# Layer norm's scales made later on POOL, stored 17 steps behind the residual sum, and read back in a stage of their own

## The chip, the core and the metric

The kernel runs on one core of one Trainium2 chip. The metric is the device time of one execution in microseconds. A core has TensorE (PE, matmuls), VectorE (DVE), ScalarE (ACT), GpSimd (POOL) and SyncE (SP), which here only issues transfers. Each engine works through its own instructions in the order in which the program emits them, so an instruction that waits holds all that stand behind it on its engine.

## What is computed

A transformer block on 2048 tokens of width 1024 in fp32: layer norm, linear attention with a learned feature map (32 heads of 32), output projection `wo` and residual sum; then layer norm, an up projection to 3584, ReLU, a down projection and a second residual sum.

```python
x = A_x
h = x + _A_ref(_layernorm(x, axis=-1), A_wqkv, A_w_phi, A_wo)
h2 = h + _B_ref(_layernorm(h, axis=-1), B_w1, B_w2)

def _layernorm(x, axis=-1, eps=1e-5):
    m = jnp.mean(x, axis=axis, keepdims=True)
    v = jnp.var(x, axis=axis, keepdims=True)
    return (x - m) / jnp.sqrt(v + eps)

def _B_ref(x, w1, w2):
    h = jnp.maximum(jnp.einsum("bsd,df->bsf", x, w1), 0)
    return jnp.einsum("bsf,fd->bsd", h, w2)
```

The case is about the second layer norm, that of `h`.

## The kernel before, in words

**Precision.** Every large operand is split into a high and a low part, and each product is three matmuls (`mm3`, L181 to L183). ACT makes the high part of a weight (L124), DVE or POOL the low part (L128).

**Order of work.** The program is a list of *items*, each some matmul groups: the key and value projections, the query projections, 32 items of the output projection (`wo_item`, 8 steps each), then the items of the up projection (4 steps each) and of the down projection. A *step* is one group of three matmuls. Everything beside the matmuls is put into a table by hand: `when(step, f, ...)` emits `f` behind the matmuls of that step. What stands under one step keeps the order in which it was entered: attention first, then the output projection, then the layer norm. `Units.advance` adds weight loads and splits at each step, as buffers come free. Below, steps are counted from the first item of the output projection; the up projection begins at step 256.

**Attention beside the output projection.** Units of the attention go two by two every 16 steps. SP loads both units' features (`at_load`, L528, tile qe: steps 63, 79, 95, 111, 127, 143, 159). POOL multiplies them with the sums of keys (L560, tile ez), DVE reduces (L566), POOL makes denominators (L576, L580), DVE inverts (L583), POOL scales (L593, L598), DVE transposes (L604), and TensorE multiplies with the key-value matrix (`at_num`, L618: steps 62, 78, 94, 110, 126 and so on; the transposes stand 10 and 7 steps before). ACT copies the result out as the high part (L625), DVE makes the low part (L636), into oT, from which the output projection reads four tiles of 128 tokens at a time.

**Output projection.** Item n of 32 is one tile and one half of the 1024 columns. SP loads that part of `x` (L643, tile xh, four buffers), DVE adds it to the product (L669) at step 8n + 9, and takes statistics of it (L680, L683). SP stores the sum to DRAM (L672, tile hd) at 8n + 14. With a tile's second half, POOL makes the layer norm's scale and bias (`ln_power`, L230 to L232) two steps behind the sum, and SP stores these two numbers per token (`wo_scale`, L688, tile scd) five steps behind the sum.

**Second layer norm.** `ln_pair` takes two tiles of tokens, 512 apart. Stage 0: for each tile and each of four groups of 32 partitions, SP reads back the scales (L698, tile scx, 1 KB) and then the rows in another layout (L699, tile xin, 128 KB); sixteen transfers in turn. Tile xin has two buffers. Stage 1: ACT applies scale and bias, four instructions for each tile (L706). Stages 2 and 3: DVE transposes each tile (L709). Stage 4: DVE makes a sum and a difference of the two tiles (L713, L714). Stage 5: POOL makes two more (L718, L719). Then `ln_store` stores seven arrays (L728, tile hs), the inputs of the up projection's seven products. `h_load` reads them (L736, tile hT), ACT and DVE split them (L744, L748).

There are eight pairs. The four of the first 1024 tokens (b = 0) run beside the output projection, pair i from step 64 + 40 i on; the four others (b = 1) beside the first half of the up projection, pair i from 60 + 68 i behind its start. The offsets of the stages are in `LN2`: with (5, 14, 18, 20, 22, 24, 30), pair 0 loads at 69, goes through ACT at 78, DVE at 82, 84 and 86, POOL at 88 and is stored from 94 to 97.

**Up projection.** Each item multiplies one weight block with one of the seven inputs into a bank of PSUM; ACT drains some banks (L771), DVE adds others (L774), then ACT and DVE do the ReLU and the combinations (L777, L780, L783), and SP stores them (L786).

Of the kernel before, what the change touches and what calls it, by code (L numbers as in the profile page):

```python
# [139 lines left out]
def kernel(  # L140
# [12 lines left out]
    v, act, pool, pe, sp = nc.vector, nc.scalar, nc.gpsimd, nc.tensor, nc.sync  # L153
# [34 lines left out]
    def do(n, k, f, *args):  # L188
        at[n, k].append((f, args))
# [8 lines left out]
    scd = [dram.tile([P, 2], F32, name=f"scd{t}") for t in range(NT)]  # L198
# [9 lines left out]
    xin, xst, xnt = {}, {}, {}  # L208
# [481 lines left out]
    def ln_pair(b, i, stage):  # L690

        tiles = [HT * b + 4 * r + i for r in range(2)]
        if stage == 0:
            for r, t in enumerate(tiles):
                xnt["h", t] = x = lnp.tile([P, D], F32, name="xin")
                for a in range(4):
                    rows = slice(32 * a, 32 * (a + 1))
                    sp.dma_start(scx[rows, 2 * i + r], scd[t].rearrange("(g t) s -> t g s", g=4))  # L698
                    sp.dma_start(x[rows].rearrange("p (c g k) -> p c g k", c=8, g=4),  # L699
                                 hd[t].rearrange("(g t) (c a k) -> a t c g k", g=4, a=4, k=32)[a])  # L700
        elif stage == 1:
            for r, t in enumerate(tiles):
                x = xnt["h", t].rearrange("p (c g k) -> p c g k", c=8, g=4)
                for g in range(4):
                    sc = scx[:, 2 * i + r, g]
                    act.activation(x[:, :, g], x[:, :, g], AF.Identity, bias=sc[:, 1:2], scale=sc[:, 0:1])  # L706
        elif stage in (2, 3):
            x = xnt["h", tiles[stage - 2]]
            v.transpose(x, x)  # L709
        elif stage == 4:  # L710
            x1, x2 = (xnt["h", t] for t in tiles)
            sums[b, i] = s12 = (mp or hp).tile([P, 2, 512], F32, name="s12", bufs=1)
            v.tensor_add(s12[:, 0, :], x2[:, 0:512], x2[:, 512:])  # L713
            v.tensor_sub(x2[:, 0:512], x1[:, 0:512], x2[:, 0:512])  # L714
        elif stage == 5:
            x1, s12 = xnt["h", tiles[0]], sums[b, i]
            s4 = (mp or hp).tile([P, 512], F32, name="s4l", bufs=1)
            pool.tensor_tensor(out=s12[:, 1, :], in0=s12[:, 0, :], in1=x1[:, 0:512], op=ALU.subtract)  # L718
            pool.tensor_tensor(out=s4, in0=x1[:, 512:], in1=s12[:, 1, :], op=ALU.subtract)  # L719
            sums[b, i] = s12, s4  # L720
# [178 lines left out]
    def when(step, f, *args):  # L899

        if step < 8 * first_up:
            do(step // 8, step % 8, f, *args)
        else:
            do(first_up + (step - 8 * first_up) // 4, step % 4, f, *args)
# [138 lines left out]
    for (t, hf), n in order:  # L1043
        do(max(n - 1, wo_first), -1, wo_load, t, hf)
        added = 8 * n + (11 if n < wo_first + 2 else 9)
        when(added, wo_add, t, hf)
        when(added, wo_stats, t, hf)
        if hf == 1:
            when(added + 2, ln_power, ("h", t))
            when(added + 5, wo_scale, t)  # L1050
        when(8 * n + (10 if n > order[-3][1] else 14), wo_store, t, hf)

    LN2 = ((5, 14, 18, 20, 22, 24, 30), (0, 14, 20, 24, 28, 32, 42))
    wo0 = 8 * wo_first
    up0 = 8 * first_up
    for i in range(4):
        for stage in range(6):
            when(wo0 + 64 + 40 * i + LN2[0][stage], ln_pair, 0, i, stage)  # L1060
            when(up0 + 60 + 68 * i + LN2[1][stage], ln_pair, 1, i, stage)
        for j in range(7):
            when(wo0 + 64 + 40 * i + LN2[0][6] + j // 2, ln_store, 0, i, j)
            when(up0 + 60 + 68 * i + LN2[1][6] + j, ln_store, 1, i, j)
    assert wo_n[8, 0] + 10 < first_up

    def up_step(b, p, m):
# [53 lines left out]
    scx = consts.tile([P, HT, 4, 2], F32, name="scx")  # L1121
# [16 lines left out]
    for i in range(4):  # L1138
        r = slice(32 * i, 32 * (i + 1))
# [76 lines left out]
```

## Time and profile before

| | us |
|---|---|
| median of 3 runs | 1953.69 |
| lowest, highest | 1952.56, 1957.18 |
| the profiled execution | 1965.29 |
| its span, first to last instruction | 1963.5 |
| its mean granted TensorE clock | 0.985 of full speed |

The profile is one execution, recorded by the hardware. Each line of its groups gives the source line, the engine, the operation and the names of the tiles as out<-in. A line of the waits reads: who waited <- for whom: us in total, times, longest. A line of the timeline gives start, duration, engine, line and tiles, and in brackets how long the engine was idle before and what ended that. SPq is SP's queue, whose durations are those of issuing a transfer and not of the transfer. A wait for several things is put down to the one that came last.

### The profile page before, as it was taken

The page shows a single profiled execution, that of the slowest core. Times are in us where ns is not written, and L with a number is a line of the kernel's source. Part 1 is how long each engine was busy: PE and PEld are TensorE (multiplying, and loading weights), DVE is VectorE, ACT ScalarE, POOL GpSimd, SP SyncE. Part 2 cuts the span into 40 slices and gives each one's busy share as a digit, 9 for nine tenths or more (in the row PEclk, how much of TensorE's full clock was granted, in tenths as well). Part 3 has the DMA queues.
Part 4 walks back from the last instruction along what each step waited for, and adds up shares of the span by engine and source line. Part 5 has one row for each costly group of instructions (what it writes and reads, how often), then busy time and mean ns, then how long its engine had stood idle before and what let it go on. Part 6 is the DMA issues. An engine that isn't in the chain of part 4 may idle for free. (4 is left out here: it accounts for less than half of the span.)

```text
span 1963.5 us, 31404 instructions
## 1 busy us (share of the span) xinstructions
PE 1902.4 (97%) x11288; PEld 1559.5 (79%) x11288; DVE 1058.3 (54%) x1673; ACT 754.0 (38%) x1334; POOL 969.6 (49%) x961
## 2 busy tenths in 40 slices
PE   9999999999999988978999999999999999999999
PEld 7888788877787766757777888888888888888887
DVE  6666578667589866455444655443343343334333
ACT  5433335222233121134444555444444444444442
POOL 4776752889856867432322322222244444444443
PEclk9999999999999989989999999999999999999999
DMA  6888786666675687797878897665677677877765
GB/s 219 272 272 266 229 272 208 196 196 196 198 236 164 176 188 174 176 256 212 238 223 242 267 305 220 198 210 175 195 247 220 209 217 235 259 215 216 214 215 177
DMA packets 368475, 432.22 MB, mean 220 GB/s; under 512 B 102208, under 2 KB 228160, under 8 KB 368320
## 3 DMA queue, kind: packets, MB, share of 16 engines
q1 hardware_dynamic: 351424, 413.45, 70.5%
q10 hardware_dynamic: 16896, 16.78, 2.5%
q8 instruction: 88, 1.44, 0.3%
q14 instruction: 67, 0.55, 0.1%
HBM read 292.75 MB, written 137.38 MB: 219 GB/s over the span
## 5 line engine op out<-in xcount | busy, mean ns | idle before, releaser
L128 POOL TENSOR_TENSOR w<-raw,w 128x512 fp32r<-128x512 f32 x355 | 473.1, 1334 | 751.9 <-ACT w L124 700.0
L124 ACT ACTIVATE w<-raw 128x512 fp32r<-128x512 f32 x686 | 409.2, 626 | 475.6 <-PE mm L183 212.0
L128 DVE TENSOR_TENSOR w<-raw,w 128x512 fp32r<-128x512 f32 x331 | 274.9, 831 | 545.2 <-ACT w L124 537.3
L181 PE MATMUL mm<-w,xT 128*128 128x512 f32 x768 | 311.0, 405 | 0.0
L182 PE MATMUL mm<-w,xT 128*128 128x512 f32 x768 | 300.7, 392 | 4.6 <-POOL w L128 3.5
L183 PE MATMUL mm<-w,xT 128*128 128x512 f32 x768 | 299.7, 390 | 0.0
L181 PE MATMUL mm<-hT,w 128*128 128x512 f32 x672 | 266.2, 396 | 24.4 <-ACT hT L744 11.1
L182 PE MATMUL mm<-hT,w 128*128 128x512 f32 x672 | 265.5, 395 | 3.2 <-DVE hT L748 3.2
L183 PE MATMUL mm<-hT,w 128*128 128x512 f32 x672 | 264.7, 394 | 0.0
L348 POOL TENSOR_TENSOR b<-b 128x256 f32<-128x256 f32 x224 | 181.5, 810 | 89.9 <-DMA b<-in_w_dram 73.8
L182 PEld LDWEIGHTS mm<-w,xT 128*128 128x128 f32 x768 | 144.5, 188 | 36.0 <-POOL w L128 6.8
L181 PEld LDWEIGHTS mm<-hT,w 128*128 128x128 f32 x672 | 128.4, 191 | 54.3 <-ACT hT L744 11.9
L181 PEld LDWEIGHTS mm<-w,xT 128*128 128x128 f32 x768 | 144.4, 188 | 30.6 <-issue 1.8
L183 PEld LDWEIGHTS mm<-w,xT 128*128 128x128 f32 x768 | 144.2, 188 | 30.7
L182 PEld LDWEIGHTS mm<-hT,w 128*128 128x128 f32 x672 | 128.3, 191 | 31.0 <-DVE hT L748 4.2
L181 PE MATMUL mm<-w 128*128 128x512 f32 x392 | 152.5, 389 | 0.0
L182 PE MATMUL mm<-w 128*128 128x512 f32 x392 | 152.5, 389 | 0.0
L183 PE MATMUL mm<-w 128*128 128x512 f32 x392 | 152.5, 389 | 0.0
L183 PEld LDWEIGHTS mm<-hT,w 128*128 128x128 f32 x672 | 128.4, 191 | 26.9
L183 PEld LDWEIGHTS mm<-w 128*128 128x128 f32 x392 | 73.6, 188 | 15.3
L182 PEld LDWEIGHTS mm<-w 128*128 128x128 f32 x392 | 73.6, 188 | 15.3
L181 PEld LDWEIGHTS mm<-w 128*128 128x128 f32 x392 | 73.6, 188 | 15.2
(159 smaller groups left out, 3147.0 us busy)
## 6 DMA issues: line engine op xcount, KB each, us to landing
raw<-t SPq DMA_DIRECT2D x224, 256.0 KB, 4.2
raw<-ad SPq DMA_DIRECT2D x196, 256.0 KB, 3.0
raw<-in_w_dram SPq DMA_DIRECT2D x168, 256.0 KB, 3.1
b<-in_w_dram SPq DMA_DIRECT2D x56, 512.0 KB, 4.1
t<-b SPq DMA_DIRECT2D x56, 512.0 KB, 4.3
ad<-c SPq DMA_DIRECT2D x112, 256.0 KB, 3.5
ad<-s SPq DMA_DIRECT2D x84, 256.0 KB, 4.1
ed<-qe ACTq DMA_DIRECT2D x32, 512.0 KB, 4.9
```

Source lines behind the costliest of these rows:

```text
L124: nc.scalar.activation(w[:, 0, :], raw[1], AF.Copy)
L128: eng.tensor_tensor(out=w[:, 1, :], in0=raw[1], in1=w[:, 0, :].bitcast(F32), op=ALU.subtract)
L181: pe.matmul(ps, a_hi, b_hi, start=first, stop=False, skip_group_check=more)
L182: pe.matmul(ps, a_hi, b_lo, start=False, stop=False, skip_group_check=more)
L183: pe.matmul(ps, a_lo, b_hi, start=False, stop=last, skip_group_check=more)
L348: pool.tensor_tensor(out=tsum[j, *out], in0=tsum[j, *a], in1=tsum[j, *b], op=ALU.subtract)
```

## The change

The scales are made four steps behind the sum instead of two, and stored 17 behind it instead of five. The pair's stage 0 loads only the rows; a new stage 1 loads the scales; the later stages are numbered one higher. For b = 0, pair 0 gets offsets of its own (rows at 70, scales 84, ACT 91, DVE 93, 94 and 96, POOL 97, stores 100 to 103), and the others begin five steps earlier and end six later (rows 0, scales 8, ACT 20, DVE 25, 27, 29, POOL 31, stores from 36). For b = 1 the scales are loaded 4 steps behind the rows, and everything from ACT on is four steps later.

```diff
                 for a in range(4):
                     rows = slice(32 * a, 32 * (a + 1))
-                    sp.dma_start(scx[rows, 2 * i + r], scd[t].rearrange("(g t) s -> t g s", g=4))
                     sp.dma_start(x[rows].rearrange("p (c g k) -> p c g k", c=8, g=4),
                                  hd[t].rearrange("(g t) (c a k) -> a t c g k", g=4, a=4, k=32)[a])
         elif stage == 1:
+            for r, t in enumerate(tiles):
+                for a in range(4):
+                    sp.dma_start(scx[32 * a:32 * (a + 1), 2 * i + r], scd[t].rearrange("(g t) s -> t g s", g=4))
+        elif stage == 2:
...
-            when(added + 2, ln_power, ("h", t))
-            when(added + 5, wo_scale, t)
+            when(added + 4, ln_power, ("h", t))
+            when(added + 17, wo_scale, t)
...
-    LN2 = ((5, 14, 18, 20, 22, 24, 30), (0, 14, 20, 24, 28, 32, 42))
+    LN2 = ((0, 8, 20, 25, 27, 29, 31, 36), (0, 4, 18, 24, 28, 32, 36, 46))
     wo0 = 8 * wo_first
     up0 = 8 * first_up
     for i in range(4):
-        for stage in range(6):
-            when(wo0 + 64 + 40 * i + LN2[0][stage], ln_pair, 0, i, stage)
+        first, ln2 = wo0 + 64 + 40 * i, LN2[0] if i else (6, 20, 27, 29, 30, 32, 33, 36)
+        for stage in range(7):
+            when(first + ln2[stage], ln_pair, 0, i, stage)
             when(up0 + 60 + 68 * i + LN2[1][stage], ln_pair, 1, i, stage)
         for j in range(7):
-            when(wo0 + 64 + 40 * i + LN2[0][6] + j // 2, ln_store, 0, i, j)
-            when(up0 + 60 + 68 * i + LN2[1][6] + j, ln_store, 1, i, j)
+            when(first + ln2[7] + j // 2, ln_store, 0, i, j)
+            when(up0 + 60 + 68 * i + LN2[1][7] + j, ln_store, 1, i, j)
```

More of the change, by code (lines that the diff above doesn't have):

```diff
@@ L706, in ln_pair @@
                     act.activation(x[:, :, g], x[:, :, g], AF.Identity, bias=sc[:, 1:2], scale=sc[:, 0:1])
-        elif stage in (2, 3):
-            x = xnt["h", tiles[stage - 2]]
+        elif stage in (3, 4):
+            x = xnt["h", tiles[stage - 3]]
             v.transpose(x, x)
-        elif stage == 4:
+        elif stage == 5:
             x1, x2 = (xnt["h", t] for t in tiles)
@@ L714, in ln_pair @@
             v.tensor_sub(x2[:, 0:512], x1[:, 0:512], x2[:, 0:512])
-        elif stage == 5:
+        elif stage == 6:
             x1, s12 = xnt["h", tiles[0]], sums[b, i]
```

## The prediction

> **What bounds the kernel now.** I read the page's head first: TensorE is busy for nearly the whole span.
>
> ```profile
> span 1963.5 us, 31404 instructions
> PE 1902.4 (97%) x11288; PEld 1559.5 (79%) x11288; DVE 1058.3 (54%) x1673; ACT 754.0 (38%) x1334; POOL 969.6 (49%) x961
> ```
>
> So the order and amount of matmuls set the end, and a change beside them is worth only what TensorE loses. The change touches no matmul; it must work through TensorE's gaps. The second view is the table of busy time in 20 us stretches (PE, PEld, DVE, ACT and POOL busy time, then granted clock, DMA share, GB/s). These six rows are those where TensorE is worst:
>
> ```profile
> 700.00:720.00 20.00, 14.03 (x144) 11.03 (x144) 11.05 (x19) 2.88 (x8) 10.85 (x14) 0.83 0.88 289
> 720.00:740.00 20.00, 17.34 (x295) 13.71 (x302) 13.05 (x23) 5.38 (x12) 13.98 (x19) 0.83 0.81 127
> 740.00:760.00 20.00, 14.95 (x109) 11.38 (x96) 13.72 (x23) 1.21 (x4) 18.07 (x23) 0.83 0.64 162
> ...
> 780.00:800.00 20.00, 15.89 (x179) 12.31 (x178) 11.06 (x16) 5.37 (x12) 12.03 (x15) 0.83 0.56 155
> ...
> 860.00:880.00 20.00, 12.73 (x42) 9.66 (x43) 10.57 (x15) 6.26 (x9) 10.00 (x16) 0.76 0.93 225
> 880.00:900.00 20.00, 15.04 (x57) 11.56 (x55) 5.32 (x6) 9.89 (x15) 3.95 (x5) 0.84 0.90 217
> ```
>
> There are two losses in each: TensorE stands idle, and its clock is granted at less than 1 for a while. All six lie where the output projection and the second layer norm run (to about 862 us) or where the up projection begins. The third view, TensorE's waits, names the causes, first from 620 to 860 us, then from 860 to 1130 us:
>
> ```profile
> PE tp L618 <- DVE qe L604: 12.0, 3, 6.3
> PE mm L183 <- DVE oT L636: 5.7, 2, 5.1
> ```
>
> ```profile
> PE mm L181 <- ACT hT L744: 11.1, 2, 8.3
> PE mm L181 <- DVE c L774: 6.3, 2, 4.2
> PE mm L181 <- DVE xh L669: 4.8, 1, 4.8
> PE mm L182 <- DVE hT L748: 3.2, 2, 2.7
> PE mm L181 <- ACT c L771: 2.2, 1, 2.2
> ```
>
> The attention's own products (L618) wait for a transpose on DVE, the projection for DVE's low parts, the up projection for its inputs hT. None of these is slow by itself; each is late because its engine or its load was queued behind the layer norm. Step by step, from the queue of SP (start, duration), the first pair of tiles:
>
> ```profile
> 681.11 0.42 SPq L698 DMA_DIRECT2D scx<-scd  x1
> ...
> 696.34 0.56 SPq L699 DMA_DIRECT2D xin<-hd  x1
> ...
> 699.16 1.09 SPq L528 DMA_DIRECT2D qe<-ed  x2
> ```
>
> Sixteen transfers, scales and rows in turn, hold SP for 696.34 + 0.56 - 681.11 = 15.8 us. Two things follow. The second tile's rows come last, so ACT and then DVE wait with everything behind them (ACT, then DVE):
>
> ```profile
> 699.59 2.07 ACT L706 ACTIVATE xin<-xin,scx 128x256 f32<-128x256 f32 x4 [3.28 <-DVE qe L604]
> ```
>
> ```profile
> 701.70 1.25 DVE L709 STREAM_TRANSPOSE xin<-xin 128x1024 f32<-128x1024 f32 x1 [2.98 <-ACT xin L706]
> ...
> 704.31 1.24 DVE L604 STREAM_TRANSPOSE qe<-qe 128x1024 f32<-128x1024 f32 x1
> ```
>
> DVE's L604, which L618 waits for, stands behind L709 in program order: this is the 6.3 us wait. And the qe load at 699.16 was behind the block, so POOL starved:
>
> ```profile
> 708.46 2.54 POOL L560 TENSOR_TENSOR ez<-qe,zb 128x512 f32<-128x512 f32 x2 [11.66 <-DMA qe<-ed]
> ```
>
> What POOL then does late makes the next transposes and L636 late. SP itself is held by POOL as well (SP's waits from 650 to 900 us):
>
> ```profile
> SPq L688 <- POOL qtz L576: 31.6, 4, 10.6
> SPq L643 <- DMA hd<-xh: 15.7, 8, 5.6
> SPq L688 <- POOL sc L232: 14.2, 4, 7.7
> ```
>
> L688 stores the scales. It stands three steps behind their making on POOL (L230 to L232), and POOL runs late: 45.8 us of waiting on SP, with hd stores and qe and xh loads queued behind. POOL late makes SP late, which makes qe late, which makes POOL late.
>
> **The change, part by part.** One step is three matmuls, by this piece of the chain of waits 3 x 0.23 = 0.69 us:
>
> ```profile
> 1060.64 0.23 PE mm L181
> ```
>
> No instruction is added or removed; each DMA, ACT and POOL instruction keeps its price, which I cost at nothing.
>
> *Scales on POOL, two steps later.* The same three small operations. They wait a little less for DVE. I take 0 for TensorE; the bounds are plus and minus 1.4 us, two steps once.
>
> *Scale store, twelve steps later (from 5 to 17 behind the sum).* 12 x 0.69 = 8.3 us more room, against a longest L688 wait of 10.6. I take most of the 45.8 us on SP as gone. What is late next on SP: the hd stores' sums and L643 (15.7 us), which stays. The scale must now land before its read: for the first pair the second tile's store is at step 74 and the read at 84, 6.9 us.
>
> *Rows and scales apart.* The eight row loads come first; the eight scale loads follow 14 steps later in the first pair, 8 in the others, 4 in the second half of the tokens. The block of 15.8 us becomes two, each between 4.5 (8 x 0.56, the row load above) and 7.9 us (half of it); I take 5, near the row. The qe load passes between: in the first pair it stands at step 79, between 70 and 84; in the second at 111, between 104 and 112.
>
> *ACT and DVE later.* In the first pair ACT moves from 78 to 91 and DVE's transposes from 82/84 to 93/94. The attention's transposes at 84 and 87, for L618 at 94, now come ahead of them. The next ones are at 100 and 103, for L618 at 110, and have slack. In the third pair the order likewise turns in their favour. In the second pair ACT's 124 stands two steps ahead of the copies of L618 at 126, which L636 needs, and TensorE needs that at about step 134. If ACT waits there, 2 us or so stay.
>
> **Output projection.** Now: idle 12.0 + 5.7 = 17.7 us; clock, four slices at 0.83, 4 x 20 x 0.17 = 13.6, of which I put 2.6 under the idle itself: 11. Together 29. I leave three waits of 2 us, at the second pair and where POOL is full, and one slow-clock period of 3.4: 9. **Gain 20**, between 0 (POOL remains the pace) and 29.
>
> The Trainium skill ("TensorE: Matmul & The Clock Gate", section "What's actually happening") says that the clock is halved after an idle window of about 3.4 us. By that rule waits of 2 us would cost no clock, and this gain would be 23.4 us; the rows above, where waits of 4 to 6 us go with 0.83, agree as far as they reach.
>
> **Start of the up projection.** Idle 11.1 + 4.8 + 3.2 = 19.1, clock 20 x (0.24 + 0.16) = 8: 27 us. Its inputs follow the last pair's stores (SP, start and duration):
>
> ```profile
> 848.98 0.82 SPq L728 DMA_DIRECT2D hs<-xin  x1
> ...
> 854.20 1.06 SPq L736 DMA_DIRECT2D hT<-hs  x2
> ```
>
> The change plans these stores six steps (4.1 us) later but spares SP the wait in front of them, since the row loads begin at 184 instead of 189 (3.5 us) and scale stores no longer hold the queue. I take SP as 5 us ahead of its place now and the first wait, 8.3, as shrinking by that. The rest is loads at a DMA share of 0.90 to 0.93, and stays. **Gain 5**, between -8 (six steps late and once more with a queue) and 15.
>
> **Second half of the tokens.** Here ACT stands at step 14 behind its loads, 9.7 us, and is not fed in time:
>
> ```profile
> 933.56 2.08 ACT L706 ACTIVATE xin<-xin,scx 128x256 f32<-128x256 f32 x4 [3.06 <-DMA scx<-scd]
> 939.29 2.08 ACT L706 ACTIVATE xin<-xin,scx 128x256 f32<-128x256 f32 x4 [3.65 <-DMA ad<-s]
> ```
>
> ```profile
> 941.96 1.28 POOL L128 TENSOR_TENSOR w<-raw,w 128x512 fp32r<-128x512 f32 x1 [13.25 <-ACT w L124]
> ```
>
> The weight splits and the drains L771 and L774 queue behind ACT: 6.3 + 2.2 = 8.5 us of TensorE. The change puts ACT at 18, 2.8 us later; SP's sixteen transfers end no later. The waits of 3.06 and 3.65 mostly go. **Gain 7**, between 0 and 8.5.
>
> Sum: 20 + 5 + 7 = 32 us. The profiled execution took 1965.3 us (span 1963.5), so it would take 1933. The median of the three runs is 1953.7, 11.6 us less. I take that difference to lie in these same waits, 29 + 27 + 8.5 = 64.5 us in the profile, so 52.9 without it, or 0.82 of it. 32 x 0.82 = 26, and **1953.7 - 26 = 1928 us**. The bounds of the three terms, all good: 52 x 0.82 = 43, 1911; all bad: +8, 1962.
>
> **Rivals.**
>
> *Given back at the up projection: 1944.* The output projection gains its 20 us, but the hT loads behind it are bound by transfers, not by SP, and TensorE merely arrives earlier and waits. For it: the DMA share of 0.93 and 0.90. Against: only 0.56 at 780 to 800, so the transfers too are delayed by SP. About 12 us would be left, x 0.82 = 10.
>
> *It does not do what it says: 1954.* POOL's own work is the pace of the output projection (18.07 of 20 us at 740 to 760), and less waiting on SP reaches nobody. Against: 11.66 us of POOL idle in one wait for qe.
>
> *SP waits for landings instead: 1965, slower.* The landing times of the tiles hs, qe and scx (min/median/max):
>
> ```profile
> DMA to landing us min/median/max: 3.7/6.0/9.4
> ```
>
> ```profile
> DMA to landing us min/median/max: 6.4/7.3/9.2
> ```
>
> ```profile
> DMA to landing us min/median/max: 2.4/3.1/8.6
> ```
>
> A row load overwrites the tile from which the pair before stores its sums (hs), since the ring has two tiles. Now the last store stands twelve steps ahead of the next row load (97 to 109), 8.3 us, more than 6.0. After the change it is one step: 103 to 104, 143 to 144, 183 to 184, and 223 to 224 for hT. SP would wait 6.0 - 0.7 = 5.3 us four times, 21 us, with qe loads, hd stores and xh loads behind it. If all of that reaches TensorE, the first two gains vanish and only the 7 remain: (21 - 7) x 0.82 = 11. It decides if qe lands later than POOL asks for it: at the second pair qe's step is seven ahead of its use, 4.8 us, and it takes 7.3. Against it: qe waits now behind 15.8 us; a wait of 5.3 and a block of 5 come to 10.3, beginning 5 steps earlier.
>
> The Trainium skill ("DMA: Bandwidth & Descriptors", section "Anatomy of one DMA — SWDGE (gpsimd) path") speaks for this rival: the wait is served by the issuing sequencer before it dispatches, and a transfer counts as done only when its last byte is confirmed in memory, longest for HBM. Its fit of 2.0 us and bytes over 436 GB/s, made for another issuing engine, gives an estimate of 2.6 us for 256 KB, so 1.9 us each time; the 6.0 us measured here differs and decides.
>
> **How the numbers follow.** Forecast 0.60, given back 0.17, no effect 0.08, slower 0.15. A measurement of this kernel can tell about 0.3% (5.9 us) from no change. Faster by more: 0.77, within: 0.08, slower: 0.15. The likeliest is 1928. The range goes from 1910, nearly all terms good, to 1958, with the given-back and no-effect cases and without the slower one.
>
> **What would show it.** Right: the L688 waits on POOL nearly gone; POOL's wait for qe well under 11 us; the waits of L618 and L636 under 9 us together; no 0.83 in three of the four slices; ACT's L706 hardly waiting after 900 us. Wrong: SP waits of 5 us or more at row loads for hs, repeated; an hT wait longer than 8.3; ACT's L706 ahead of the copies at the second pair, with L636 late by more than 5 us.

## The result: 10.4 us faster, less than half of the forecast

| | before | after |
|---|---|---|
| median of 4 runs, us | 1954.15 | 1943.76 |
| lowest, highest | 1952.56, 1957.18 | 1942.16, 1946.88 |
| the profiled execution | 1965.29 | 1944.36 |
| its mean granted TensorE clock | 0.985 | 0.988 |

The ratio of the times is 0.9947 [0.9929, 0.9965]. A second set of runs of the same two kernels gave 0.9939 [0.9925, 0.9953]. The forecast was 1928 us, or 26 us less than before; the time lies in its range, but 16 us above it.

The head of the page of after answers to that of before:

```profile
span 1942.6 us, 31377 instructions
PE 1897.2 (98%) x11288; PEld 1558.0 (80%) x11288; DVE 1066.1 (55%) x1673; ACT 753.5 (39%) x1334; POOL 977.4 (50%) x961
```

The two profiles differ by 20.9 us, twice what the medians do, since the profiled execution of before was 11 us above its median and that of after is not. So the profiles may say where time went, and only the timed runs how much.

The 20 us stretches of after (PE, PEld, DVE, ACT, POOL busy, granted clock, DMA share, GB/s), the four of the output projection that were shown of before:

```profile
700.00:720.00 20.00, 13.68 (x176) 10.71 (x175) 14.35 (x24) 5.73 (x15) 15.89 (x18) 0.88 0.75 234
720.00:740.00 20.00, 18.78 (x198) 14.88 (x196) 12.23 (x25) 5.85 (x15) 16.07 (x28) 0.95 0.83 175
740.00:760.00 20.00, 16.79 (x181) 12.81 (x182) 18.21 (x28) 1.22 (x4) 18.23 (x21) 0.83 0.82 246
780.00:800.00 20.00, 16.20 (x190) 12.62 (x183) 14.12 (x26) 2.38 (x8) 15.54 (x23) 0.84 0.73 208
```

The output projection keeps two stretches at 0.83 and 0.84. The up projection begins some 14 us sooner in after, so its start is compared by stage: the 50 us from the last start of the output projection's products (read below), before and then after:

```profile
852.90:902.90 50.00, 30.94 (x107) 23.45 (x106) 20.73 (x27) 20.86 (x31) 16.67 (x19) 0.77 0.94 239
```

```profile
842.70:892.70 50.00, 40.96 (x158) 32.33 (x157) 26.11 (x34) 24.73 (x37) 19.58 (x20) 0.90 0.99 261
```

TensorE is busy for 10 us more of these 50, and its clock is higher; 9 us of idle time are left. TensorE's waits from 620 to 860 us, then from 860 to 1130 us:

```profile
PE tp L618 <- DVE qe L604: 7.6, 3, 3.2
PE tp L618 <- issue: 5.7, 2, 3.5
PE mm L181 <- ACT hT L747: 4.4, 1, 4.4
PE mm L181 <- ACT oT L625: 1.2, 1, 1.2
```

```profile
PE mm L181 <- DVE c L777: 5.5, 2, 3.4
PE mm L181 <- ACT c L774: 3.4, 1, 3.4
PE mm L182 <- DVE hT L751: 3.0, 1, 3.0
PE mm L181 <- ACT hT L747: 0.9, 1, 0.9
```

The lines of the layer norm are shifted: ACT's split of hT is L747 (L744 before), DVE's is L751 (L748), the drains are L774 and L777 (L771 and L774). ACT's part of the wait for hT fell from 11.1 to 4.4 + 0.9 = 5.3 us, DVE's hardly (3.2 to 3.0); L618 still waits 7.6 + 5.7 = 13.3; the drains, which the change should have freed, still cost 8.9 (8.5 before).

Last the stages, from the rows that give the first and the last start of the products that read oT and hT. Before:

```profile
L181 PE MATMUL mm<-w,oT x160: 389/389/794, 622.3 to 848.8; 128*128 128x512 f32 x160
...
L181 PE MATMUL mm<-wf,oT x96: 389/389/795, 650.1 to 852.9; 128*128 128x512 f32 x96
```

```profile
L181 PE MATMUL mm<-hT,w x672: 389/389/796, 862.0 to 1425.6; 128*128 128x512 f32 x168
```

The output projection takes 852.9 - 622.3 = 230.6 us (O), then TensorE needs 862.0 - 852.9 = 9.1 to the first product with hT (W), and the up projection takes 1425.6 - 862.0 = 563.6 (U). By the same rows after has O 220.7, W 5.2 and U 556.8:

```profile
L181 PE MATMUL mm<-hT,w x672: 387/389/794, 847.9 to 1404.7; 128*128 128x512 f32 x168
```

### The profile page after: what moved, and what is told of

It reads as the page before. It is cut to its first block, busy times and chain, and to the rows that moved or that the text cites. A ratio compares the mean times of both kernels' runs of the same rounds, so it can differ in the third digit from the quotient of the medians.

```text
span 1942.6 us, 31377 instructions
## 1 busy us (share of the span) xinstructions
PE 1897.2 (98%) x11288; PEld 1558.0 (80%) x11288; DVE 1066.1 (55%) x1673; ACT 753.5 (39%) x1334; POOL 977.4 (50%) x961
## 4 chain that ended last, share of the span: by engine, by line
PE 74%; DMA 7%; POOL 7%; issue 5%; DVE 3%; SPq 3%; ACT 1%; POOLq 0%; DVEq 0%; ACTq 0%
PE mm L181 18%; PE mm L182 18%; PE mm L183 18%; PE ac L183 3%; PE ac L181 3%; PE ac L182 3%; PE tp L183 2%; PE tp L181 2%; PE tp L182 2%; POOL w L128 2%; SPq L698 2%; POOL b L348 1%; PE tp L276 1%; DMA qe<-ed 1%; POOL ez L560 1%
## 5 line engine op out<-in xcount | busy, mean ns | idle before, releaser
L128 POOL TENSOR_TENSOR w<-raw,w 128x512 fp32r<-128x512 f32 x355 | 478.7, 1350 | 733.6 <-ACT w L124 678.9
L181 PEld LDWEIGHTS mm<-hT,w 128*128 128x128 f32 x672 | 128.4, 191 | 43.2 <-DVE c L777 6.4
```

Of the source, the lines that this page charges most:

```text
L128: eng.tensor_tensor(out=w[:, 1, :], in0=raw[1], in1=w[:, 0, :].bitcast(F32), op=ALU.subtract)
L181: pe.matmul(ps, a_hi, b_hi, start=first, stop=False, skip_group_check=more)
```

## The experiments

Theory A: SP's one queue is the price. The time for which the rows and the scales hold SP, and the order in which it issues them, decides when the loads behind them go out; the later store frees that queue, the split fills it again. Theory B, the rival: the transfers are the price. The rows move in pieces of 128 bytes, the transfer engines are the limit, and SP's order matters little.

All times stand against runs of before on the same chip; before itself differs by up to 5 us from set to set, so kernels of different sets are compared by their ratios. O, W and U are of one profiled execution each, and two executions of one kernel differ in U by about 4 us (before and after appear twice).

| kernel | us | before | ratio | O | W | U |
|---|---|---|---|---|---|---|
| before | | | | 230.6 | 9.1 | 563.6 |
| before, again (e10) | 1961.05 | 1958.85 | one run | 229.7 | 10.1 | 559.4 |
| after | 1943.76 | 1954.15 | 0.9947 [0.9929, 0.9965] | 220.7 | 5.2 | 556.8 |
| after, again (e9) | 1947.11 | 1958.85 | 0.9939 [0.9925, 0.9953] | 219.3 | 4.8 | 560.9 |
| second half undone (e1) | 1939.33 | 1955.45 | 0.9919 [0.9905, 0.9934] | 218.5 | 5.9 | 553.2 |
| store undone (e2) | 1957.97 | 1955.45 | 1.0014 [1.0006, 1.0023] | 223.0 | 11.0 | 560.8 |
| later store alone (e12) | 1942.72 | 1958.85 | 0.9920 [0.9906, 0.9933] | 222.1 | 3.8 | 556.9 |
| pairs 1 to 3 joined (e6) | 1948.97 | 1956.84 | 0.9953 [0.9940, 0.9966] | 226.7 | 5.2 | 561.4 |
| second half, scales first (e3) | 1935.29 | 1955.45 | 0.9899 [0.9884, 0.9915] | 220.7 | 4.5 | 553.3 |
| the same, earlier (e11) | 1936.29 | 1958.85 | 0.9883 [0.9866, 0.9900] | 220.9 | 7.4 | 547.6 |
| second half in turn, ACT late (e7) | 1938.57 | 1956.84 | 0.9905 [0.9892, 0.9919] | 220.6 | 5.4 | 552.1 |
| scales first everywhere (e8) | 1939.47 | 1956.84 | 0.9912 [0.9898, 0.9925] | 223.9 | 3.8 | 554.5 |
| rows issued by ACT (e5) | 1964.23 | 1956.84 | 1.0039 [1.0025, 1.0053] | 246.4 | 0.7 | 555.1 |
| rows in 4 KB pieces (e4) | 1918.63 | 1955.45 | 0.9814 [0.9800, 0.9827] | 211.4 | 1.3 | 549.8 |
| the same, first half only (e14) | 1932.53 | 1957.39 | 0.9875 [0.9861, 0.9888] | 213.9 | 1.9 | 557.6 |
| scale loads twice (e13) | 1962.51 | 1957.39 | 1.0030 [1.0019, 1.0042] | 234.8 | 8.0 | 559.3 |
| both (e15) | 1946.46 | 1957.39 | 0.9957 [0.9941, 0.9974] | 216.9 | 8.2 | 558.3 |

The kernels e4, e14 and e15 leave out the layout that the later products need, and so compute something else; all others compute the same. Several times lie outside what was expected of them: e1 and e4 below every range, e2, e13 and (by 0.7 to 1.5 us) e12, e6 and e15 above that of theory A, e5 and e8 outside both; e11 is taken up at its place.

### Which part of the change gains: e1, e2, e12, e6

e1 gives the second half of the tokens (b = 1) its old order and offsets:

```diff
                     rows = slice(32 * a, 32 * (a + 1))
+                    if b == 1:
+                        sp.dma_start(scx[rows, 2 * i + r], scd[t].rearrange("(g t) s -> t g s", g=4))
...
-            for r, t in enumerate(tiles):
+            for r, t in enumerate(tiles if b == 0 else ()):
...
-    LN2 = ((0, 8, 20, 25, 27, 29, 31, 36), (0, 4, 18, 24, 28, 32, 36, 46))
+    LN2 = ((0, 8, 20, 25, 27, 29, 31, 36), (0, 0, 14, 20, 24, 28, 32, 42))
```

> The changed kernel with only the second half of the tokens put back as before: there the scale and row loads alternate again and ACT stands 14 steps behind them. Theory A: the change's part in the second half gave nothing, because eight row loads in a row hold SP for about 9 us (not 5) and the scales now come behind them, so ACT waits about 8 us in one piece where it waited 3 and 3.7; expected 1942 to 1946 us, like the changed kernel. Rival: ACT four steps later gave 5 to 7 us, as the prediction had it; expected 1949 to 1951 us.

Measured 0.9919: undoing that part does not lose its forecast gain of 7 x 0.82 = 5.7 us but gains 0.0020 to 0.0028 of the time, 4 to 5.5 us. Each of the two differences alone is at the edge of what its intervals allow; U supports it. The eight kernels here that have after's second half (after, e9, e2, e5, e6, e13, e14, e15) have a mean U of 558.8 us, the three with the later store and the loads in turn (e1, e12, e7) 554.1. Before and e10 load in turn too and have 563.6 and 559.4, but there TensorE is busy for only 29.2 and 31.2 of the first 40 us of U (35.3 in after), so their U also holds the late start.

e2 undoes the store:

```diff
-            when(added + 4, ln_power, ("h", t))
-            when(added + 17, wo_scale, t)
+            when(added + 2, ln_power, ("h", t))
+            when(added + 5, wo_scale, t)
```

> The changed kernel with only the making and the storing of the scales put back (2 and 5 steps behind the sum). If SP's waiting for POOL at the scale store was what cost time before, most of the 10 us is lost again: 1950 to 1954 us, with about 40 us of SP waits at L688. If the gain came from the order and the later place of the pairs, and SP is held by its row loads either way: 1942 to 1946 us.

Measured 1.0014: without the later store nothing is left of the gain, and 0.0067 x 1954 = 13.1 us are lost against after. SP's waits from 650 to 900 us in e2, and TensorE's wait for hT:

```profile
SPq L688 <- POOL sc L232: 28.1, 5, 8.8
SPq L688 <- POOL qtz L576: 15.1, 3, 6.9
```

```profile
PE mm L181 <- ACT hT L747: 10.2, 1, 10.2
```

That is the wait of before, 43.2 us at one instruction, and the largest part of the loss comes out in W (11.0 for 5.2). In after, these are SP's waits in the same stretch that stand for it and for the rival "SP waits for landings":

```profile
SPq L688 <- POOL sc L230: 0.8, 1, 0.8
...
SPq L698 <- DMA hs<-xin: 0.3, 1, 0.3
```

L688 waits 0.8 us for the scales, 1.4 with two shorter waits for POOL, and the row loads (L698) wait 0.3 us for the stores of the pair before. But the scale loads (L703), which now stand by themselves, wait, by the profile, for landings of transfers issued before them. In the first pair:

```profile
SPq L703 <- DMA xh<-in_x_dram: 2.0, 1, 2.0
SPq L703 <- DMA qe<-ed: 1.9, 2, 1.0
SPq L703 <- DMA scd<-sc: 1.2, 1, 1.2
```

With 0.4 for hd these are 5.5 us, and in the four pairs beside the output projection 10.1 us (3.1 for qe, 2.4 each for xh and scd, 1.4 for xin, 0.8 for hd). In before the loads of rows and scales together waited 2.7 us there. Only scd is read by a scale load; why it waits for the others no run here shows.

e12 is the other side: the kernel before with the later making and store of the scales and no split. Pair 0 needs offsets that leave room for its store:

```diff
-            when(added + 2, ln_power, ("h", t))
-            when(added + 5, wo_scale, t)
+            when(added + 4, ln_power, ("h", t))
+            when(added + 17, wo_scale, t)
...
+        ln2 = LN2[0] if i else (14, 27, 29, 30, 32, 33, 36)
...
-            when(wo0 + 64 + 40 * i + LN2[0][stage], ln_pair, 0, i, stage)
+            when(wo0 + 64 + 40 * i + ln2[stage], ln_pair, 0, i, stage)
```

> The kernel before with only the later scales (4 and 17 steps behind the sum) and the first pair moved to where its scales exist (loads, still alternating, at 78; the rest at 91 to 100 as in the changed kernel). If the scale store is the whole gain and the split is worth nothing: 1937 to 1942 us, like the changed kernel with its second half as before. If the split is needed for it: 1948 us or more.

Measured 0.9920, the same as e1: the later store gives the gain, 15.6 us, and the split of the first half adds nothing that can be measured. (e12 also moves the first pair, which its later store requires; e2, with the change's own offsets, shows no gain from offsets alone.) e6 joins scales and rows again in pairs 1 to 3 of after:

```diff
                     rows = slice(32 * a, 32 * (a + 1))
+                    if b == 0 and i:
+                        sp.dma_start(scx[rows, 2 * i + r], scd[t].rearrange("(g t) s -> t g s", g=4))
...
-            for r, t in enumerate(tiles):
+            for r, t in enumerate(() if b == 0 and i else tiles):
```

> The changed kernel with the split undone in pairs 1 to 3 of the first half of the tokens: scale and row loads alternate again, where the rows now stand. Theory A: alternating, a row load and a scale load together take about 1.3 us, so the scales cost SP little beside the rows; the block is 12 to 16 us in one piece with qe behind it, against 9 and 5 with qe between. Expected within 4 us of the changed kernel, either way: 1940 to 1948 us. Rival (the split itself is what gained in the first half): 1950 us or more.

Measured 0.9953 beside 0.9947 and 0.9939 of after: the same within the intervals.

### Why the second half loses: e3, e7, e11

SP's queue at the first pair of the second half, and ACT's instructions that apply the scales (start, duration; in brackets ACT's idle time before and what ended it). After:

```profile
901.93 9.51 SPq L698 DMA_DIRECT2D xin<-hd  x8
...
913.76 4.37 SPq L703 DMA_DIRECT2D scx<-scd  x8
```

```profile
918.98 4.04 ACT L709 ACTIVATE xin<-xin,scx 128x256 f32<-128x256 f32 x8 [7.95 <-DMA scx<-scd]
```

e1, in turn:

```profile
898.48 1.06 SPq L699 DMA_DIRECT2D scx<-scd  x1
...
909.95 0.56 SPq L700 DMA_DIRECT2D xin<-hd  x1
```

```profile
907.35 2.08 ACT L711 ACTIVATE xin<-xin,scx 128x256 f32<-128x256 f32 x4 [2.16 <-DMA scx<-scd]
```

In turn, the sixteen transfers hold SP for 909.95 + 0.56 - 898.48 = 12.0 us, and after half of them ACT has its first tile: it starts 907.35 - 898.48 = 8.9 us behind the first load. Apart, the two blocks hold SP for 9.51 + 4.37 = 13.9 us and end 16.2 us behind their start, and no tile can begin before the second block has begun to land: ACT starts 17.1 us behind the first load, later by more than the 4 steps that it was given, and waits 8 us in one piece.

e3 turns the blocks round, the scales eight steps ahead of the rows:

```diff
-    LN2 = ((0, 8, 20, 25, 27, 29, 31, 36), (0, 4, 18, 24, 28, 32, 36, 46))
+    LN2 = ((0, 8, 20, 25, 27, 29, 31, 36), (0, -8, 18, 24, 28, 32, 36, 46))
```

> The changed kernel with one number changed: in the second half of the tokens the scales are loaded 8 steps ahead of the rows instead of 4 behind. Theory A (scales late because they queue behind the row loads on SP): ACT's wait at L709 after 900 us falls from 24 us in total to under 8, TensorE's waits there from 8.9 us to under 3, time 1934 to 1938 us. Rival (the rows themselves, or the transfers as a whole, are what is late): ACT waits for the rows instead, 1942 to 1945 us.

Measured 0.9899, 8 to 9 us below after, with intervals that don't touch. One edit of one number: the same transfers, in the other order. The time is as theory A has it, its two other marks were missed. ACT's waits from 895 to 1100 us are now for rows, as in the rival, 16.1 us (under 8 were expected, 23.9 were in after) and in pieces of 5 us at most, where ACT waited 8 us in one piece in after; TensorE's waits for the drains are 5.7 us (under 3 were expected, 8.9 were in after):

```profile
ACT xin L709 <- DMA xin<-hd: 16.1, 7, 5.1
```

e7 keeps the loads in turn and gives ACT the later place alone: e1's first two edits, and

```diff
-    LN2 = ((0, 8, 20, 25, 27, 29, 31, 36), (0, 4, 18, 24, 28, 32, 36, 46))
+    LN2 = ((0, 8, 20, 25, 27, 29, 31, 36), (0, 0, 18, 24, 28, 32, 36, 46))
```

> The changed kernel whose second half of the tokens loads scales and rows in turn as before, but keeps ACT and what follows four steps later. This is the prediction's term by itself, ACT 2.8 us later and SP's sixteen transfers no later. Theory A (the later ACT was worth something and the order of the loads took it away and more): under the 1939 us of the kernel with the whole second half as before, 1932 to 1936 us. Rival (the later place is worth nothing): 1938 to 1941 us.

Measured 0.9905 beside e1's 0.9919: 2.7 us for the later place, with intervals that overlap, so it is not clear of nothing, and 1938.6 us is the rival's time. ACT's waits before the scales are applied fall only from 22.8 us in e1 to 19.6, and TensorE's for the drains from 9.2 to 6.9. e11 is e3 with rows and scales both eight steps earlier:

```diff
-    LN2 = ((0, 8, 20, 25, 27, 29, 31, 36), (0, 4, 18, 24, 28, 32, 36, 46))
+    LN2 = ((0, 8, 20, 25, 27, 29, 31, 36), (-8, -16, 18, 24, 28, 32, 36, 46))
```

> The changed kernel with, in the second half of the tokens, the rows 8 and the scales 16 steps earlier than ACT's place allows for now (rows at -8, scales at -16, ACT still at 18). Theory A (ACT waits there only because a block of eight row loads takes 9 us to issue and 4 to land): ACT's waits for rows, 16 us in the kernel with the scales first, go to about 0, and the 5.5 us of TensorE waiting for L777 with them; 1928 to 1932 us. Rival (the waits for L777 come from DVE's own queue or from the transfers' load): 1934 to 1937 us.

Measured 0.9883, the lowest of the kernels that do the whole work: 22.6 us below before, and by 0.0036 x 1954 = 7 us below e1, with intervals that don't touch (e3's overlaps). In microseconds, 1936.3, this is the rival's range; its set has the slowest before, and at the 1954 us of the first set the ratio gives 1931, theory A's. ACT's waits for rows went from 16.1 to 6.2 us, not to about 0. TensorE's wait for DVE's drains from 900 to 1130 us, 5.5 us in after, is then

```profile
PE mm L181 <- DVE c L777: 2.1, 1, 2.1
```

So taking ACT's waits at L709 away, with the drains behind it, is worth about the 7 us that the forecast put them at: the drains cost 2.3 us of TensorE here and 9.2 in e1. But it takes loads that start earlier, scales first; ACT four steps later (e7) is not enough, and the change as it stands collects nothing.

### Queue or transfers: e4, e5, e13, e14, e15, and e8

e4 loads the rows in pieces of 4 KB, in both halves, without the other layout:

```diff
-                    sp.dma_start(x[rows].rearrange("p (c g k) -> p c g k", c=8, g=4),
-                                 hd[t].rearrange("(g t) (c a k) -> a t c g k", g=4, a=4, k=32)[a])
+                    sp.dma_start(x[rows], hd[t][rows])
```

> The changed kernel with the row loads taken as whole 4 KB rows instead of 128-byte pieces, the same bytes (the layout that the later products need is not made, so the result is another). Theory A (SP is held because eight loads in small pieces back to back cannot be issued faster than they are worked off): a block of eight falls from 9 us to 5 or less, qe loads and scales come 4 us earlier for each pair, 1925 to 1934 us. Rival (the output projection goes at POOL's pace, or waits for landings of the pair stored just before): the block may shrink, but the time stays at 1940 us or more.

Measured 0.9814, with the best O of all and a U near e11's. That the rows are costly is clear, but not by what: larger pieces shorten both the transfers and SP's issuing. e5 meant to tell them apart by letting ACT issue the rows of the first half:

```diff
-                    sp.dma_start(x[rows].rearrange("p (c g k) -> p c g k", c=8, g=4),
+                    (sp if b else act).dma_start(x[rows].rearrange("p (c g k) -> p c g k", c=8, g=4),
```

> The changed kernel with the row loads of the first half of the tokens issued by ACT, which has little to do there, instead of SP; the same transfers in the same small pieces. Theory A (SP's queue is what a block of row loads costs): SP goes on to scales and qe at once, TensorE's waits at L618 fall from 13 us to under 5, time 1930 to 1938 us. Rival B (the transfer engines need that long for 8192 small pieces, whoever issues them): scales and qe land as late as before, and ACT's own copies at L625 now queue behind the loads; 1942 to 1950 us.

Measured 1.0039, slower than before and than both ranges: theory A's number failed, but the experiment had a fault of its own. The issuing holds ACT far longer than it held SP (14.9 to 26.6 us for each pair's eight loads), so the copies of L625 behind it came late and TensorE waited 16.0 us for them. ACT's queue in e5 and TensorE's wait:

```profile
679.00 25.93 ACTq L698 DMA_DIRECT2D xin<-hd  x7
```

```profile
PE mm L181 <- ACT oT L625: 16.0, 1, 16.0
```

It speaks for neither theory. So the four kernels after, e13, e14 and e15 cross the two prices, in the first half alone. e13 issues each scale load twice, the second time into another pair's place: 1 KB each, 4608 more packets in all beside 368 thousand, but eight more issues for each pair. e14 has the 4 KB pieces of e4. e15 has both. The edits of e13 and of e14:

```diff
                     sp.dma_start(scx[32 * a:32 * (a + 1), 2 * i + r], scd[t].rearrange("(g t) s -> t g s", g=4))
+                    if b == 0:
+                        sp.dma_start(scx[32 * a:32 * (a + 1), (2 * i + r + 2) % 8], scd[t].rearrange("(g t) s -> t g s", g=4))
```

```diff
                     rows = slice(32 * a, 32 * (a + 1))
+                    if b == 0:
+                        sp.dma_start(x[rows], hd[t][rows])
+                        continue
```

> The changed kernel with every scale load of the first half of the tokens issued twice (the second time into a place that is overwritten later), eight more transfers of 1 KB for each pair, some 5 us more of SP's queue and hardly any work for the transfer engines. Theory A (time on SP's queue is what the pairs cost): 1949 to 1956 us beside 1944 to 1947 for the changed kernel. Rival B (the small pieces of the row loads cost by the transfer engines' time, SP's queue does not matter): within 3 us of the changed kernel.

> The changed kernel with whole 4 KB rows in the first half of the tokens alone (another layout there, so another result). The part of the 26 us of the kernel with whole rows everywhere that belongs to the first half: if the second half's part is the 11 us that earlier loads gave there, 13 to 16 us are left, 1929 to 1933 us. If the gain sits in the second half: 1940 us or more.

> Both edits of the first half together: whole rows, scale loads twice. SP's queue is then about as long as in the changed kernel, the transfer engines have the lighter work. Theory A: most of the gain of whole rows is lost, 1938 to 1945 us. Rival B: the gain stays, 1929 to 1934 us.

Measured 1.0030, 0.9875 and 0.9957, beside 0.9939 of after in the nearest set. The stretch from 680 to 820 us, in the order after, e13, e14, e15 (PE's busy time is the second number, the DMA share the last but one):

```profile
680.00:820.00 140.00, 125.45 (x1473) 99.83 (x1472) 89.69 (x147) 25.79 (x64) 91.70 (x119) 0.93 0.79 191
```

```profile
680.00:820.00 140.00, 111.04 (x1411) 87.89 (x1410) 83.71 (x142) 21.75 (x56) 90.66 (x119) 0.88 0.76 174
```

```profile
680.00:820.00 140.00, 130.60 (x1504) 104.42 (x1503) 95.98 (x155) 29.00 (x68) 95.88 (x123) 0.95 0.81 207
```

```profile
680.00:820.00 140.00, 129.77 (x1490) 103.68 (x1489) 88.58 (x148) 27.13 (x65) 89.37 (x116) 0.93 0.75 197
```

In e13 the transfer engines are busy for less of the time (0.76 for 0.79), and still the kernel loses (1.0030 - 0.9939) x 1957 = 18 us, and TensorE's longest wait is 12.6 us. Theory B does not give that. At the first pair (start and duration, SP) the second block of e13 goes from 694.33 to 708.26 + 0.43 = 708.69, 14.4 us (6.4 of them waits for landings) where after has 9.91 (5.5), and the qe load behind it leaves at 710.56 instead of 704.64:

```profile
694.33 1.16 SPq L703 DMA_DIRECT2D scx<-scd  x1
...
708.26 0.43 SPq L705 DMA_DIRECT2D scx<-scd  x1
...
710.56 0.92 SPq L528 DMA_DIRECT2D qe<-ed  x2
```

```profile
PE tp L618 <- issue: 20.1, 2, 12.6
```

In e14 the row block of that pair holds SP for 6.08 us where it held it for 9.05 in after, and the kernel gains (0.9939 - 0.9875) x 1957 = 13 us. Of the 6.08 us, 2.5 are a wait for a landing; the eight issues take 0.30 to 0.42 us each, in after 0.65 to 2.87 with no wait between them. With both edits the loss and the gain nearly cancel. The time for which SP is held is enough to explain all four; that shorter transfers give a part of e14's and e4's gain is not excluded, since SP's waits for landings depend on the transfers.

```profile
679.22 6.08 SPq L699 DMA_DIRECT2D xin<-hd  x8
```

e8 followed theory A further: scales ahead of rows in pairs 1 and 3 of the first half as well, and the store at 13:

```diff
-            when(added + 17, wo_scale, t)
+            when(added + 13, wo_scale, t)
...
+    LN2 = ((0, 8, 20, 25, 27, 29, 31, 36), (0, -8, 18, 24, 28, 32, 36, 46))
+    SCALES = (20, -10, 8, -8)
...
-            when(first + ln2[stage], ln_pair, 0, i, stage)
+            when(first + (SCALES[i] if stage == 1 else ln2[stage]), ln_pair, 0, i, stage)
```

> The changed kernel with the scales ahead of the rows wherever they exist by then (second half of the tokens 8 steps ahead; in the first half pair 1 ten steps and pair 3 sixteen steps earlier than now), and the scale store 13 behind the sum instead of 17, so that the first pair's store stands ahead of its row loads. Theory A: the first pair's scale block falls from 10 us to 5, the qe load of the second pair no longer has scales behind rows, and the second half gains its 9 us; 1927 to 1933 us. Rival (only the second half matters): 1934 to 1937 us.

Measured 0.9912, no better than e3 (0.9899), from which it differs by the store and the first half: a miss. The order of the blocks that gains in the second half shows no gain beside the output projection. But the two are mixed here: with the store at 13, L688 waits 6.7 us for POOL again (4.4 + 2.3), and the row block of the first pair held SP for 11.78 us. What the order alone does there stays open.

The last two have no edit and say how far one profile carries: e9 is the changed kernel, e10 the kernel before, each once more.

> The changed kernel itself, on the chip of the experiments beside it, for a ratio with a narrower interval. All theories: 0.992 to 0.997 of the kernel before. If it falls at 0.992, like the kernel with the second half as before, then the second half's part costs nothing; theory A says 0.995, 5 us more than that kernel.

Measured 0.9939, beside 0.9947 the first time: the gain of the change stands.

> The kernel before, for a second profiled execution: the first took 1965.3 us against a median of 1953.7. As the prediction scaled its sum, the missing 11 us should lie in TensorE's waits and slow clock in the output projection, at the start of the up projection and in its first half. Rival: they are spread over the whole span, and the factor 0.82 had no ground.

Measured 1961.05 us, with O and W as in the first profile of before and U 4.2 us shorter.

## The prediction, step by step

**The scale store: right.** "I take most of the 45.8 us on SP as gone": 1.4 us are left, e2 brings 43.2 back, and with them the loss of the whole gain.

**Output projection and start of the up projection: right in sum, a little too large, and wrongly shared out.** Together they were put at (20 + 5) x 0.82 = 20.5 us; e1, which has these two parts alone, measured (1 - 0.9919) x 1954 = 15.8. O fell by some 10 us where 20 x 0.82 = 16 were forecast; W fell by 4 to 5 us and the first stretch of U with it, by more than the 4 forecast (TensorE is busy for 10 us more of the 50 us behind O). The marks set for it say the same: the waits of L618 and L636 should have come under 9 us and are 13.3, and three of the four stretches should have left 0.83, and two did. The failure at the second pair that was allowed for, ACT ahead of the copies, cost 1.2 us (oT L625).

**"The block of 15.8 us becomes two, each between 4.5 (8 x 0.56, the row load above) and 7.9 us (half of it); I take 5": this step failed.** The price of 0.56 us was that of a row load between scale loads, and the cheapest: in that block five of the eight took it, the others 1.78, 0.66 and 1.16. And waits of a scale load for landings were put at nothing. Here are after's two blocks of the first pair with the qe load that was meant to pass between them, and ACT behind:

```profile
678.86 9.05 SPq L698 DMA_DIRECT2D xin<-hd  x8
...
691.23 0.90 SPq L528 DMA_DIRECT2D qe<-ed  x2
...
693.18 9.91 SPq L703 DMA_DIRECT2D scx<-scd  x8
...
704.64 0.91 SPq L528 DMA_DIRECT2D qe<-ed  x2
```

```profile
703.44 4.05 ACT L709 ACTIVATE xin<-xin,scx 128x256 f32<-128x256 f32 x8 [15.88 <-DMA scx<-scd]
```

The qe load passes, as forecast. But the blocks take 9.05 and 9.91 us, more together than the 15.8 of the one block before. A line of eight (x8) runs from the first start to the last end: in the first block nothing is waited for, so its 9.05 us are issuing; of the second's 9.91 us, 5.5 are the waits for landings shown above, and the issuing alone is 4.4, under the 5 forecast. In the other three pairs the row blocks hold SP for 8.7 to 10.1 us and the scale blocks for 4.8 to 6.3. The next qe load waits behind the second block. POOL's wait for qe from 650 to 1100 us, before and after, went only to a half:

```profile
POOL ez L560 <- DMA qe<-ed: 32.0, 6, 11.7
```

```profile
POOL ez L560 <- DMA qe<-ed: 16.0, 4, 8.0
```

This goes with the split of the first half being worth nothing by itself (e12, e6), and with the time for which SP is held deciding the rest (e13 to e15). The Trainium skill ("DMA: Bandwidth & Descriptors", section "Issuing engines are not separate DMA queues") says that issuing from several engines saves only the time on the sequencer, usually small beside the transfer. Here SP's time was the price, by e13, issuing and waits together; and e5 shows that another engine is no free place for it.

**"The change puts ACT at 18, 2.8 us later; SP's sixteen transfers end no later": failed.** They end 16.2 us behind their start where e1 shows 12.0, and in an order in which all the rows must be issued before the first scale is there, without which ACT cannot begin. A gain of 7 x 0.82 = 5.7 us became a loss of 4 to 5.5. Two things were wrong. The missed point was what ACT's first instruction needs: the scales, now behind eight row loads. And with the loads in turn as the forecast had them (e7), "the waits of 3.06 and 3.65 mostly go" did not hold either: 19.6 of e1's 22.8 us stay, and the gain is 2.7 us at the median, not clear of nothing. What the waits are worth was sized rightly: with the scales ahead, and both early, e11 gains 7 us over e1. Of the 26 - 10.4 = 15.6 us that are missing, about 10 to 11 are this, and 20.5 - 15.8 = 4.7 lie in the output projection and the start of the up projection. That the blocks' price is the reason there is argued, not shown alone; for it is e14, which with shorter row blocks there gains 13 us over after.

**The factor 0.82** put the 11.6 us by which the profile of before exceeded the median into these same waits. A second profile of before, at 1961.05 us, doesn't show that: it has waits of the same size (from 620 to 862, and from 862 to 1130 us), and where the excess lay stays open. The 4.2 us between the two profiles lie in U.

```profile
PE tp L618 <- DVE qe L604: 14.0, 3, 6.3
```

```profile
PE mm L181 <- ACT hT L744: 13.1, 2, 9.3
```

**The rivals.** "Given back at the up projection" gave about the right time, 1944, for a reason that did not occur: the wait at its start fell (W from 9 to 10 us to 5). That its time fits is luck. "SP waits for landings instead" did not occur where it was expected, 0.3 us at L698, but in part at the scale loads: 10.1 us at L703. "It does not do what it says" fell with L688.

## What to carry to other kernels

Price a block of transfers by a block of the same kind, since a transfer issued between others of another size has another price, and ask of each consumer which load it needs first and last. And add what a transfer may wait for in front of its issue. Here one later store gave all the gain; the change's regrouping of sixteen transfers gave nothing in one half and a loss in the other, where another order of the same transfers gained. Test the parts of a change alone, since two parts of opposite sign look like one small gain.

## What the runs showed of the hardware

- A row load of 1024 pieces of 128 bytes holds SP for 0.56 us in most cases between two scale loads (five of eight in before's first pair), but eight in a row hold it for 8.7 to 10.1 us in after's first half, 1.1 to 1.3 us each on average, with hardly a wait between them (0.3 us in the four pairs). As 32 pieces of 4 KB one holds it for 0.30 to 0.42 us (e14, first pair). Issued by ACT, seven of the small pieces hold it for 25.9 us (e5). So the time grows with the number of pieces here; why a load costs more among its like is not settled.
- SP also waits, by the profile, in front of 1 KB loads for landings of earlier transfers: 5.5 us of the 9.91 in after's first scale block, 4.3 of them for transfers that the loads do not read.
- The clock was granted at half for 6.8 us behind one wait of 2.17 us. The Trainium skill ("TensorE: Matmul & The Clock Gate", section "What's actually happening") has the clock halved after an idle window of about 3.4 us, by which waits of 2 us would cost no clock, as the prediction noted; this trace shows otherwise. In after, TensorE waits 2.17 us, runs 32 short products in half a microsecond, and waits 1.63 us:

```profile
793.39 0.34 PE L618 MATMUL tp<-qe,kvL 32*32 32x128 f32 x8 [2.17 <-issue]
...
795.54 0.47 PE L618 MATMUL tp<-qe,kvL 32*32 32x128 f32 x8 [1.63 <-DVE qe L604]
```

The granted clock falls before the second wait is more than begun, and is whole again at 800.6:

```profile
793.70:793.90 0.20, 0.20 (x29) 0.00 (x0) 0.00 (x0) 0.00 (x0) 0.20 (x1) 0.71 0.95 195
...
800.50:800.80 0.30, 0.30 (x3) 0.26 (x2) 0.27 (x2) 0.00 (x0) 0.00 (x0) 0.82 0.84 131
```

A mean of 0.71 over 0.2 us is full clock for 0.08 us and half for the rest, so it falls at 793.8, while the second wait runs from 793.9 to 795.5; by the same working it rises at 800.6. Between them every stretch read has 0.50.
